# Normalised rows of batches 2 to 7 transposed by DMA instead of by TensorE: attention followed by a normalised MLP, one core of Trainium2

## The chip, the core and the metric

The kernel runs on one core of one Trainium2 chip. A core has TensorE (matmuls and weight loads), DVE (VectorE), ACT (ScalarE), POOL (GpSimd) and SP (SyncE, which issues most of the DMAs). The metric is device time in microseconds of one execution, lower is better. A profiled execution has a span, from its first to its last instruction, and a time of its own that is a little longer.

## The reference, cut to what matters

```
B, H, S, D = 8, 8, 576, 64
scores = q @ k.T / sqrt(D) + min(-(cum_i - cum_j), 0), causal     # cum: running sum of max(s, 0)
attn   = exp(scores - max) / sum
x      = (attn @ v), heads side by side                           # [8, 576, 512]
xn     = (x - mean(x)) / sqrt(var(x) + 1e-6) * g_ln
out    = x + max(xn @ w_ch1, 0) @ w_ch2                           # w_ch1 [512, 2048], w_ch2 [2048, 512]
```

All inputs and the output are float32. The first MLP matmul contracts over the 512 columns of xn, so TensorE needs xn with these columns on the partitions: xn has to be transposed. Attention works in bf16 copies, and so does the MLP.

## The kernel before, in words

**Tiling.** A batch has 576 rows: four tiles of 128 and a rest of 64. The rests of two batches share a tile of 128, so an odd batch has five tiles to normalise and an even batch four; the four shared tiles of all batches make one more chunk of 512 rows at the very end (xTm, "mixed rows"). A tile of xn is [128 rows, 512] in bf16. Its transpose is four blocks of 128 x 128, and for a batch they form xT, [128, 4, 512]: kd counts the blocks of the contraction, the 512 columns are the batch's rows.

**The loop.** One loop runs over n = 8 b + h, batch b and head h (lines 745 to 834). The schedule is written by hand: each engine executes its instructions in the order in which the program lists them. A round n from 16 on does, in order: pre(n), which issues loads, casts and row transposes for later heads; scores(n), matmuls into `sa`, `sb`, `sc` with an exponential on ACT and a causal mask on POOL; one or two units of MLP work with `scores_d` between them; pv(n - 2), attention times v for the head two rounds back; then transposes of xn where the round has them; then further units.

**MLP units.** `queue` holds the MLP of one batch as 32 units: 16 of `mlp1` (line 493: four matmuls `ph` of 128 x 512 that read all 512 columns of xT, followed by a ReLU into hT) and 16 of `mlp2` (four units to a row tile; the fourth ends with `yo` on DVE, line 524, and an output DMA on SP, line 542). The queue is emptied at the end of round 8 b + 3, and the units of batch b - 1 are put in. So the first `ph` of batch b - 1 comes right after the scores of round 8 b + 4, that is of head 4.

**From attention to xT.** Head 7 of batch b - 1 is finished by pv in round 8 b + 1. Then DVE makes the statistics and the tiles xn one after the other (`ln_xn`, line 444; five buffers). In round 8 b + 2 TensorE transposes tiles 0 and 1, in round 8 b + 3 tiles 2 to 4 (`ln_tr`, line 478): four transposes into a PSUM tile `trx` and one copy from there to xT. The copy is on DVE for b = 3 to 7, and on ACT for batch 1 and batch 7. Between the tiles single units run. xT has two buffers, used by turns.

**After the loop.** Batch 7 has its own ending (lines 835 to 842): the last two pv, then for each tile t: xn of tile t + 1, one unit of batch 6, the transposes of tile t. The rest of batch 6's units follow (four), then the MLP of batch 7 and that of the mixed rows, with nothing beside them.

**SP's queue.** SP issues in program order and waits in order. In it stand the loads of v (line 139) and of rows of k and q (line 164), each into one of six staging buffers that a cast on POOL empties; the DMA transposes of these rows into kq (`tr_rows`, line 182), which the scores of batches 3 to 7 read; and the outputs (line 542), each of which waits for its yo. In round 8 b + 2, pre(n) puts one row transpose, four row loads and one v load into it, the units of the round an output; in round 8 b + 3, pre(n) puts four more row loads and a v load.

Of the kernel before, what the change touches and what calls it, by code (L numbers as in the profile page):

```python
# [15 lines left out]
P = 128  # L16
# [3 lines left out]
def kernel(  # L20
# [11 lines left out]
    nc = tc.nc  # L32
    B, H, S, D = q.shape
# [5 lines left out]
    NF = S // P  # L39
# [48 lines left out]
    xTm = const.tile([P, KD, 512], BF16, name="xTm")  # L88
# [7 lines left out]
    def copy_on(eng, out, in_):  # L96
        if eng == "act":
            nc.scalar.copy(out=out, in_=in_)  # L98
        elif eng == "dve":
            nc.vector.tensor_copy(out=out, in_=in_)  # L100
        else:
            nc.gpsimd.tensor_copy(out=out, in_=in_)  # L102
# [27 lines left out]
    def ld_cast_pair(g):  # L130
        ld_cast("k", g)
        ld_cast("q", g)
# [12 lines left out]
    def ld_cast_v(b, t):  # L145
        pn = P if t < NF else TL
        nc.gpsimd.dma_start(
            out=v_bf[b % 2][:pn, t, :, 0:D],
            in_=v[b, :, t * P : t * P + pn, :].rearrange("h s d -> s h d"),
        )  # L150
# [45 lines left out]
    def ld_w1(c):  # L196
        sl = slice(c * 512, (c + 1) * 512)
        nc.gpsimd.dma_start(out=w1_bf[:, :, sl], in_=w1_r[:, :, sl])

    def ld_w2(i):  # L200
        nc.gpsimd.dma_start(
            out=w2_bf[:, 4 * i : 4 * i + 4, :], in_=w2_r[:, 4 * i : 4 * i + 4, :]
        )
# [3 lines left out]
    def aug(gam, eng, h0=0):  # L207
        r = slice(gam * G + h0, gam * G + G)
        i = gam % 2
        eng.dma_start(out=kq[i][D : D + 1, 1, h0:G, 0:S], in_=c_hi[r, :])  # L210
        for j in range(3):
            eng.dma_start(out=kq[i][D + 1 + j : D + 2 + j, 0, h0:G, 0:S], in_=c3[r, j, :])
# [215 lines left out]
    xTs = {}  # L428
    xns = {}
# [48 lines left out]
    def ln_tr(b, t, eng="dve"):  # L478
        if (b, t) not in xns:
            return  # L480
        xn = xns.pop((b, t))
        tr = ps_t.tile([P, KD, P], BF16, name="trx", tag="tr")
        for kd in range(KD):
            nc.tensor.transpose(tr[:, kd, :], xn[:, kd * P : (kd + 1) * P], ident)  # L484
        if t < NF:
            dst = xTs[b][:, :, t * P : (t + 1) * P]
        else:
            dst = xTm[:, :, (b // 2) * P : (b // 2 + 1) * P]
        copy_on(eng, dst, tr)

    first_unit = [False]

    def mlp1(xT, fb):
# [63 lines left out]
    def run_units(n, dve_first=False):  # L557
        for i in range(n):
            if queue:
                first_unit[0] = dve_first and i == 0  # L560
                queue.pop(0)()
# [33 lines left out]
    for i in range(2):  # L595
# [5 lines left out]
        out=maskT,  # L601
        in_=maskT,
# [18 lines left out]
    for t in range(NT):  # L621
# [5 lines left out]
        out=c_in, in0=c_in, scalar1=0.0, scalar2=1.0 / scale, op0=ALU.max, op1=ALU.mult  # L627
    )
    nc.vector.tensor_tensor_scan(
        out=c_sc, data0=c_one, data1=c_in, initial=0.0, op0=ALU.mult, op1=ALU.add  # L630
# [44 lines left out]
    def pre(n):  # L675
        if n == 0:
            nc.vector.memset(mhalf, -0.5)
            ld_cast_pair(4)
        elif n == 1:
            ld_w1(1)  # L680
        elif n == 3:
            ld_cast_pair(5)
            for t in range(NT):
                ld_cast_v(1, t)
        elif n == 4:
            ld_w1(2)
            ld_w1(3)
        elif n == 7:
            ld_cast_pair(6)
            ld_w2(0)  # L690
            ld_cast_pair(7)
            ld_w2(1)
        elif n == 10:
            ld_w2(2)
            ld_w2(3)
        elif n == 12:
            nc.vector.memset(cT[:, :, 0, :, 0], -1.0)
            nc.vector.memset(cT[:, :, 1, :, 1:4], 1.0)
        elif n == 16:
            for r in rows:  # L700
                nc.gpsimd.memset(r[:, :, :, KA:P], 0.0)
        if n in PAIR_LOADS:
            ld_cast_pair(PAIR_LOADS[n])
        if n % 4 == 0 and 2 <= n // 4 + 1 < 2 * NPE:
            aug(n // 4 + 1, nc.sync)
        for gam in range(2 * NPE, NG):
            m = n - 4 * gam
            if m == -6:
                ld_rows(gam, 0), ld_rows(gam, 1)
            elif m == -5:  # L710
                cast_rows(gam, 0), cast_rows(gam, 1)
                ld_rows(gam, 2), ld_rows(gam, 3)
            elif m == -4:
                tr_rows(gam, 0), tr_rows(gam, 1)
                cast_rows(gam, 2), cast_rows(gam, 3)
                ld_rows(gam, 4)
            elif m == -3:
                tr_rows(gam, 2), tr_rows(gam, 3)
                cast_rows(gam, 4)
            elif m == -2:  # L720
                tr_rows(gam, 4)
        for nb in range(2, B):
            m = n - H * nb + (5 if nb == 2 else 7)
            if 0 <= m < NT:
                ld_v(nb, m)
            if 1 <= m <= NT:
                cast_v(nb, m - 1, "pool")
# [16 lines left out]

    for n in range(BH):
        b, h = n // H, n % H
        pre(n)
        if n < 8:
            scores(b, h)
            if h in (1, 3, 5, 6):  # L750
                scores_d(b, h // 2)
            if h in (0, 2, 4):
                qk_pair(h // 2 + 1, ("dve", "dve"), ("act", "dve" if h < 4 else "act"))
            pend.append((b, h))
            if n == 7:
                pv_next()
                tr_pair(4)
                pv_next()
                evac_pair("k", 4, ("act", "act"))
                evac_pair("q", 4, ("act", "act"))  # L760
                trc = bias_tr()
                keep_warm(8)
                continue
            if n % 2 == 1 or n == 0:
                keep_warm(2)
            if n > 1:
                pv_next()
            if n == 6:
                pv_next()
            continue  # L770
        if n == 8:

            phs = [
                pool.tile([P, 512], F32, name="ph", tag=tag)
                for pool, tag in ((ps_m, "m"), (ps_m, "m"), (ps_s, "s"), (ps_s, "s"))
            ]

            def columns(t):
                cols = slice(t * P, (t + 1) * P)
                for fb, ph in enumerate(phs):  # L780
                    for kd in range(KD):
                        nc.tensor.matmul(  # L782
                            ph[:, cols],
                            lhsT=w1_bf[:, kd, fb * P : (fb + 1) * P],
                            rhs=xTs[0][:, kd, cols],
                            start=(kd == 0),
                            stop=(kd == KD - 1),
                        )

            for t in range(NF):  # L790
                ln_tr(0, t, "act" if t < 3 else "dve")
                if t > 0:
                    columns(t - 1)
            columns(NF - 1)
            for fb, ph in enumerate(phs):
                if fb % 2 == 0:
                    nc.scalar.activation(out=hT[:, fb, :], in_=ph, func=ACT.Relu)
                else:
                    nc.vector.tensor_scalar_max(out=hT[:, fb, :], in0=ph, scalar1=0.0)
            ln_first_rstd()  # L800
            queue += batch_units(0)[4:]
            scores(b, h)
            scores_d(b, h // 2)
            pend.append((b, h))
            run_units(1)
            continue

        end = next(m for m in (8 * i + 3 for i in range(2, B + 1)) if m >= n)
        nu = (2 if n < 16 else -(-len(queue) // (end - n + 1))) - 2
        if n in PAIRS:  # L810
            qk_pair(PAIRS[n], ("dve", "dve"), ("act", "act"))
        scores(b, h)
        run_units(1, True)
        if h % 2 == 0:
            scores_d(b, h // 2)
        run_units(1)
        if n > 9:
            pv_next()
        if n == 9:
            bias_rows(trc)  # L820
        pend.append((b, h))
        lt = {2: (0, 1), 3: (2, 3, 4)}.get(h, ()) if b > 1 else ()
        for t in lt:
            ln_tr(b - 1, t, "act" if b == 2 else "dve")
            if t != 1 and t != 4:
                run_units(1)
                nu -= 1
        if n == 2 * H + 2:
            for t in range(3, NT):
                ln_xn(1, t)  # L830
        run_units(nu)
        if b > 1 and h == 3:
            run_units(len(queue))
            queue += batch_units(b - 1)
# [4 lines left out]
    for t in range(NT):  # L839
        ln_xn(B - 1, t + 1)  # L840
        run_units(1)
        ln_tr(B - 1, t, "act")
    run_units(len(queue))
    queue += batch_units(B - 1)
    queue += mixed_units()
# [30 lines left out]
```

## Time and profile before

| what | us |
|---|---|
| median of 3 runs | 368.14 |
| lowest and highest of them | 367.79 and 369.08 |
| the profiled execution's own time | 368.74 |
| its span | 367.0 |
| DMA packets of the span | 147981, 50.42 MB, mean 137 GB/s |

How to read such a profile. The page begins with the busy time of each engine and its share of the span; PEld is TensorE's weight load, which overlaps its matmuls. Then the span is cut into 40 equal slices, with the busy share of each engine in tenths; the row DMA is the mean busy share of the core's 16 DMA engines. "The chain that ended last" follows the end of the program back from instruction to what released it, and gives shares of the span by engine and by line. A group line says: source line, engine, operation, tile written `<-` tile read, count, then durations and where it lies. In a timeline the columns are start, duration (both us), engine, source line, operation; in square brackets stands how long the engine was idle before and what ended that. SPq marks an issue of a DMA on SP: the duration is that of the issue, not of the transfer.

The costliest groups of the page beside those shown further on:

```profile
L515 PE MATMUL py<-w_bf,hT 128*128 128x512 bf16 (+1 forms) x592 | 136.5, 373 | 0.4 <-DVE yo L524 0.4
L497 PE MATMUL ph<-xT,w_bf 128*128 128x512 bf16 x496 | 117.8, 379 | 0.1
```

Both are the MLP. Matmuls are pipelined, so the mean of one (373 and 379 ns) is longer than the distance from one to the next.

### The profile page before, as it was taken

The page shows a single profiled execution, that of the slowest core. Times are in us where ns is not written, and L with a number is a line of the kernel's source. Part 1 is how long each engine was busy: PE and PEld are TensorE (multiplying, and loading weights), DVE is VectorE, ACT ScalarE, POOL GpSimd, SP SyncE. Part 2 cuts the span into 40 slices and gives each one's busy share as a digit, 9 for nine tenths or more (in the row PEclk, how much of TensorE's full clock was granted, in tenths as well). Part 3 has the DMA queues.
Part 4 walks back from the last instruction along what each step waited for, and adds up shares of the span by engine and source line. Part 5 has one row for each costly group of instructions (what it writes and reads, how often), then busy time and mean ns, then how long its engine had stood idle before and what let it go on. Part 6 is the DMA issues. An engine that isn't in the chain of part 4 may idle for free.

```text
span 367.0 us, 8372 instructions
## 1 busy us (share of the span) xinstructions
PE 357.8 (97%) x3079; PEld 198.0 (54%) x3079; DVE 205.8 (56%) x539; ACT 194.2 (53%) x371; POOL 161.3 (44%) x441
## 2 busy tenths in 40 slices
PE   8899999999999999999999999999999999999995
PEld 3577565565555555555555555555555554444444
DVE  7597789796438453944384547743675483112211
ACT  5795988568743674357534753476337522501410
POOL 8864375747553746445754562555652101000000
PEclk9999999999999999999999999999999999999999
DMA  7999995579965989599968996798730011011013
GB/s 138 170 195 175 201 204 88 116 179 173 187 140 129 236 177 189 117 227 184 192 158 203 206 188 133 183 202 183 167 102 2 0 60 57 3 56 58 3 29 86
DMA packets 147981, 50.42 MB, mean 137 GB/s; under 512 B 134185, under 2 KB 143268, under 8 KB 147940
## 3 DMA queue, kind: packets, MB, share of 16 engines
q1 hardware_dynamic: 129364, 40.74, 50.9%
q0 software_dynamic: 18176, 8.62, 20.4%
q10 hardware_dynamic: 400, 0.52, 0.5%
q8 instruction: 24, 0.39, 0.4%
q14 instruction: 17, 0.14, 0.2%
HBM read 37.11 MB, written 9.44 MB: 127 GB/s over the span
## 4 chain that ended last, share of the span: by engine, by line
PE 85%; DVE 7%; ACT 3%; DMA 2%; issue 1%; ACTq 0%
PE ph L497 32%; PE py L515 31%; PE pot L389 7%; PE sc L312 4%; PE sa L312 3%; PE sb L312 3%; DVE xn L451 2%; PE trx L484 2%; ACT er L323 2%; DMA kq<-c 1%; ACT kq L98 1%; PE trqk L255 1%; DVE stats L423 1%; PE ph L782 1%; DMA c_in<-in_s_dram 1%
## 5 line engine op out<-in xcount | busy, mean ns | idle before, releaser
L515 PE MATMUL py<-w_bf,hT 128*128 128x512 bf16 (+1 forms) x592 | 136.5, 373 | 0.4 <-DVE yo L524 0.4
L497 PE MATMUL ph<-xT,w_bf 128*128 128x512 bf16 x496 | 117.8, 379 | 0.1
L507 ACT ACTIVATE hT<-ph 128x512 bf16<-128x512 f32 x102 | 61.0, 598 | 62.8 <-PE ph L497 62.8
L515 PEld LDWEIGHTS <-hT 128*128 128x128 bf16 x592 | 53.5, 98 | 49.1 <-issue 0.9
L497 PEld LDWEIGHTS <-w_bf 128*128 128x128 bf16 x560 | 50.3, 97 | 51.7 <-issue 3.3
L323 ACT ACTIVATE er<-sa 128x512 bf16<-128x512 f32 x64 | 38.2, 597 | 70.3 <-PE sa L312 39.9
L331 POOL TENSOR_SCALAR_AFFINE_SELECT er<-er 128x128 bf16<-128x128 bf16 x216 | 58.2, 294 | 26.4 <-ACT er L323 26.3
L505 DVE TENSOR_SCALAR hT<-ph 128x512 bf16<-128x512 f32 x38 | 26.3, 692 | 54.5 <-PE ph L497 49.1
L176 POOL CAST rows<-rowtmp 128x512 bf16<-128x512 f32 (+1 forms) x50 | 30.5, 609 | 49.1 <-DMA rowtmp<-in_q_dram 48.4
L312 PEld LDWEIGHTS <-kq 68*128 68x128 bf16 x440 | 32.8, 97 | 26.5 <-DMA kq<-c 1.6
L389 PEld LDWEIGHTS <-er 128*128 128x128 bf16 x960 | 37.4, 98 | 14.2 <-issue 0.7
L389 PE MATMUL pot<-v_bf,er 128*128 128x65 bf16 x960 | 39.6, 193 | 0.1
L323 ACT ACTIVATE er<-sc 128x512 bf16<-128x512 f32 x64 | 39.1, 610 | 0.0
L397 DVE RECIPROCAL rinv<-pot 128x5 f32<-128x5 f32 x64 | 12.3, 192 | 47.5 <-PE pot L389 47.2
L323 ACT ACTIVATE er<-sb 128x512 bf16<-128x512 f32 x64 | 38.3, 598 | 0.1
L524 DVE SCALAR_TENSOR_TENSOR yo<-py,rstd,xb 128x512 f32<-128x512 f32 x32 | 23.9, 748 | 25.5 <-PE py L515 20.8
L399 DVE TENSOR_TENSOR xb<-pot,rinv 128x256 f32<-128x256 f32 x64 | 27.2, 425 | 2.2
L439 POOL TENSOR_TENSOR rstd<-rstd,mhalf 128x4 f32<-128x4 f32 (+1 forms) x8 | 8.8, 1097 | 43.8 <-DVE rstd L438 43.8
L312 PE MATMUL sa<-kq 68*128 68x512 bf16 x64 | 24.4, 381 | 1.2 <-DMA kq<-c 1.1
L423 DVE BATCH_NORM_STATS2 stats<-xb 128x6 f32<-128x128 f32 (+2 forms) x100 | 25.3, 312 | 0.4
L312 PE MATMUL sc<-kq 68*128 68x256 bf16 (+1 forms) x208 | 25.2, 232 | 0.3
L102 POOL CAST v_bf<-vtmp 128x512 bf16<-128x512 f32 (+1 forms) x30 | 18.4, 613 | 14.3 <-DMA vtmp<-in_v_dram 14.3
(101 smaller groups left out, 332.8 us busy)
## 6 DMA issues: line engine op xcount, KB each, us to landing
out_dram<-yo SPq DMA_DIRECT2D x32, 256.0 KB
vtmp<-in_v_dram SPq DMA_DIRECT2D x24, 256.0 KB
rowtmp<-in_k_dram SPq DMA_DIRECT2D x40, 128.0 KB
rowtmp<-in_q_dram SPq DMA_DIRECT2D x40, 128.0 KB
w_bf<-in_moe_w_ch_dram POOLq DMA_DIRECT2D x8, 512.0 KB, 11.1
kp<-in_k_dram POOLq DMA_DIRECT2D x11, 144.0 KB, 6.6
qp<-in_q_dram POOLq DMA_DIRECT2D x11, 144.0 KB, 7.3
v_bf<-in_v_dram POOLq DMA_DIRECT2D x8, 128.0 KB, 8.5
```

The source lines that it names most:

```text
L176: nc.gpsimd.tensor_copy(out=r[0:pn, :, :, 0:D], in_=loaded.pop(("rows", gam, t))[0:pn])
L312: nc.tensor.matmul(a[:, c + a0 - q0 : c + a1 - q0], lhsT=k_cols(b, h, kb), rhs=cols, start=True, stop=not (pe_mask and diag),)
L323: nc.scalar.activation(out=e[:, o : o + 512], in_=a, func=ACT.Exp, scale=scale)
L331: nc.gpsimd.affine_select(out=e[:, o : o + P], in_=e[:, o : o + P], compare_op=ALU.is_ge, fill=0.0, base=0, pattern=[[1, P]], channel_mult ...
L389: nc.tensor.matmul(pot[:, t, :], lhsT=e[:, o : o + P], rhs=vv[:, kb, h, :], start=(kb == 0), stop=(kb == last),)
L399: nc.vector.tensor_tensor(out=xb[b][:, :, hs], in0=pot[:, 0:NF, 0:D], in1=rinv[:, 0:NF].unsqueeze(2).to_broadcast([P, NF, D]), op=ALU.mult,)
L423: nc.vector.bn_stats(out=st[b][:, t, part, :], in_=x[:, lo:hi])
L497: nc.tensor.matmul(ph, lhsT=w1_bf[:, kd, fb * P : (fb + 1) * P], rhs=xT[:, kd, :], start=(kd == 0), stop=(kd == KD - 1),)
L505: nc.vector.tensor_scalar_max(out=hT[:, fb, :], in0=ph, scalar1=0.0)
L507: nc.scalar.activation(out=hT[:, fb, :], in_=ph, func=ACT.Relu)
L515: nc.tensor.matmul(py[0], lhsT=hT[:, fb, t * P : (t + 1) * P], rhs=w2_bf[:, fb, c0:c1], start=(fb == 0), stop=(fb == FB - 1),)
L524: nc.vector.scalar_tensor_tensor(out=yo, in0=py[0], scalar=rs, in1=x[:, c0:c1], op0=ALU.mult, op1=ALU.add)
```

## The change

A new helper `ln_dma` does what `ln_tr` does, with one DMA on SP's queue for a tile: it reads xn from SBUF and writes the transpose into xT or xTm, without PSUM and without a copy. The batches 2 to 6 use it in the loop: tiles 0 to 2 at the end of round 8 b + 2, after its units, and tiles 3 and 4 at the start of round 8 b + 3, ahead of pre(n). Batch 7 uses it in the ending, at the place of `ln_tr`. Batches 0 and 1 keep TensorE. The number of units that a round runs is the same; where single units ran between the transposes, they now run in one go.

```diff
+    def ln_dma(b, t):
+        if (b, t) not in xns:
+            return
+        if t < NF:
+            dst = xTs[b][:, :, t * P : (t + 1) * P]
+        else:
+            dst = xTm[:, :, (b // 2) * P : (b // 2 + 1) * P]
+        nc.sync.dma_start_transpose(out=dst, in_=xns.pop((b, t)))
...
     for n in range(BH):
         b, h = n // H, n % H
+        if b > 2 and h == 3:
+            ln_dma(b - 1, 3), ln_dma(b - 1, 4)
         pre(n)
...
-        lt = {2: (0, 1), 3: (2, 3, 4)}.get(h, ()) if b > 1 else ()
+        lt = {2: (0, 1), 3: (2, 3, 4)}.get(h, ()) if b == 2 else ()
         for t in lt:
-            ln_tr(b - 1, t, "act" if b == 2 else "dve")
+            ln_tr(b - 1, t, "act")
...
         run_units(nu)
+        if b > 2 and h == 2:
+            for t in range(3):
+                ln_dma(b - 1, t)
...
     for t in range(NT):
         ln_xn(B - 1, t + 1)
         run_units(1)
-        ln_tr(B - 1, t, "act")
+        ln_dma(B - 1, t)
```

## The prediction, made before the result was known

> **What bounds the kernel now.** I read the page first (busy shares, the slices, the chain that ended last), then the tiles trx and kq, then the timeline around one hand-over from a batch's last output to its next first MLP.
>
> ```profile
> PE 357.8 (97%) x3079; PEld 198.0 (54%) x3079; DVE 205.8 (56%) x539; ACT 194.2 (53%) x371; POOL 161.3 (44%) x441
> ...
> DMA  7999995579965989599968996798730011011013
> ...
> PE 85%; DVE 7%; ACT 3%; DMA 2%; issue 1%; ACTq 0%
> ```
>
> TensorE is busy 97% of the span and holds 85% of the chain: a microsecond taken from its queue is worth about one, and one in which it stands still costs one, since nothing later has slack to give it back. The DMA engines are near 90% in most slices up to three quarters of the span, then nearly idle.
>
> ```profile
> L484 PE MATMUL trx<-ident,xn x144: 217/219/230, 32.1 to 303.1; 128*128 128x128 bf16 x144
> L100 DVE COPY xT<-trx x21: 403/415/425, 35.6 to 271.7; 128x512 bf16<-128x512 bf16 x21
> L98 ACT COPY xT<-trx x11: 586/586/587, 32.6 to 302.3; 128x512 bf16<-128x512 bf16 x11
> ```
> ```profile
> L186 SPq DMA_TRANSPOSE kq<-rows x50: 1222/1274/2432, 83.0 to 267.8; - x50
> ```
>
> The first group is what goes; the second is the nearest thing to what comes: a DMA transpose holds SyncE (SP) about 1.27 us. It is of 1024 columns, and those of 64 rows, half the bytes, take the same (the one at 154.36 below), so the time hangs on the columns or is fixed.
>
> The hand-over of batch 3 (n = 34 to 36), one timeline with all engines:
>
> ```profile
> 150.72 0.39 PE L484 MATMUL trx<-ident,xn 128*128 128x128 bf16 x4
> ...
> 150.95 1.03 PE L515 MATMUL py<-w_bf,hT 128*128 128x512 bf16 x4
> ...
> 153.13 0.75 DVE L524 SCALAR_TENSOR_TENSOR yo<-py,rstd,xb 128x512 f32<-128x512 f32 x1
> ...
> 153.91 0.36 SPq L542 DMA_DIRECT2D out_dram<-yo  x1
> ...
> 154.36 1.23 SPq L186 DMA_TRANSPOSE kq<-rows  x1
> ...
> 156.25 0.50 SPq L164 DMA_DIRECT2D rowtmp<-in_q_dram  x1
> ...
> 157.35 0.51 SPq L164 DMA_DIRECT2D rowtmp<-in_q_dram  x1
> ...
> 157.90 0.51 SPq L139 DMA_DIRECT2D vtmp<-in_v_dram  x1
> ...
> 158.50 0.52 SPq L542 DMA_DIRECT2D out_dram<-yo  x1
> ...
> 159.07 0.43 SPq L164 DMA_DIRECT2D rowtmp<-in_k_dram  x1
> ...
> 159.18 1.03 PE L497 MATMUL ph<-xT,w_bf 128*128 128x512 bf16 x4
> 159.26 0.61 POOL L176 CAST rows<-rowtmp 128x512 bf16<-128x512 f32 x1 [3.10 <-DMA rowtmp<-in_q_dram]
> ...
> 160.54 0.62 POOL L176 CAST rows<-rowtmp 128x512 bf16<-128x512 f32 x1 [0.52 <-DMA rowtmp<-in_q_dram]
> ```
>
> The reader is to see three things. Four transposes of a tile hold TensorE 0.23 us (150.72 to 150.95), well below the 4 x 219 ns of the pipelined records. SP is late: held by the output at 153.91, whose yo DVE makes only after its five xn, it then issues without a pause (transpose, four row loads, one v load, output) until 159.02. And the first ph, which reads all 512 columns of xT, stands at 159.18. A load issued by 156.75 is there at 159.26 and one issued by 157.86 at 160.54: 2.5 to 2.7 us after the end of its issue, with the queue full.
>
> ```profile
> 157.90:162.50 4.60, 4.60 (x46) 2.62 (x45) 2.73 (x7) 2.33 (x6) 1.96 (x5) 1.00 1.00 248
> ...
> 269.70:275.00 5.30, 5.30 (x59) 3.20 (x58) 3.11 (x7) 1.77 (x5) 1.43 (x7) 1.00 0.28 102
> ```
>
> By stretches (the last two columns are the DMA share and GB/s): at this hand-over the DMA engines are full at 248 GB/s; at that of batch 6 they are not.
>
> [...] The trace shows the cold rate at its start, 12 matmuls in 5.13 us, 0.43 us each against 0.22 later (4 in 0.86 in the chain):
>
> ```profile
> 1.27 5.13 PE L568 MATMUL idle<-zeros 128*128 128x512 bf16 x12 [1.27 <-DVE warm L584]
> ```
>
> **The change part by part.** Tiles moved: batches 2, 4, 6 have four, 3, 5, 7 have five: 27.
>
> 1. Removed from TensorE: 27 x 4 transposes, 27 x 0.22 = 5.9 us, all on the path. Removed elsewhere: 22 copies of 0.415 us on DVE and 5 of 0.59 on ACT, beside TensorE and worth nothing by themselves (DVE is busy 56%, ACT 53%).
>
> 2. Added to SP: 27 transposes of 512 columns. Unknown duration d: 0.61 us if it goes by columns (half of 1.22), 1.27 if fixed. I take the middle, 0.95; nothing argues for an end. Bytes: 131 KB each, at 248 GB/s 0.53 us of all DMA engines, rounded up to 0.57.
>
> 3. Moved: in the loop, all five come after the output of head 2 in program order, so at 159.07 in this hand-over (call it S), in front of the row and v loads of head 3. With a full queue the work ahead is worth 2.6 us; it shrinks while SP issues more slowly than the engines drain. The fourth transpose lands at S + 4d + max(0.85, 2.6 - 4(d - 0.57)). The 0.85 is my floor: the output issued at 153.91 shows its first bytes at about 154.75 in the DMA slices. With d = 0.95: S + 4.88. With 0.61 also S + 4.88, as the engines then set the pace; with 1.27, S + 5.93.
>
> 4. The new wait: the first ph of the batch. Behind it on TensorE stands everything, in order, and the engine has nothing else to run. What this costs is landing less ph of before, and the removed transposes no longer count, for TensorE would only come to the wait earlier:
>
> | batch | S | first ph before | landing | cost |
> |---|---|---|---|---|
> | 2 | 119.83 | 120.86 | 124.71 | 3.85 |
> | 3 | 159.07 | 159.18 | 163.95 | 4.77 |
> | 4 | 197.30 | 196.90 | 202.18 | 5.28 |
> | 5 | 235.14 | 235.23 | 240.02 | 4.79 |
> | 6 | 270.25 | 272.95 | 274.90 | 1.95 |
>
> S and ph are read as above from the same view of each hand-over; batch 6 has no load left, so its landing is S + 3.8 + 0.85. Sum: +20.6 us.
>
> 5. Batch 7: SP comes to its transposes after the output of the yo at 299.03, about 300.2. Four issues end at 304.0, landing 304.85. TensorE, 5 x 0.22 = 1.1 us ahead of the 306.63 of before, wants it at 305.5. No wait: -1.1 us. The fifth goes to the mixed rows, needed much later. With d = 1.27 the landing is 306.1, and the gain 0.5.
>
> 6. The clock. The stalls are the costs above plus the 0.9 to 1.1 us that TensorE arrives early: 4.7, 5.9, 6.2, 5.9, 2.8. [...] some 2.7 drops. Each costs half of some 4.8 us in which the start of this trace ran cold (eleven of the twelve at 0.43): 2.4 us, as an estimate. +6.4, between 0 and 12.
>
> 7. SP's later loads and rows come 5d = 4.75 us later. TensorE is then as late as that, so this cover holds; if the stall vanished, the casts on POOL, with the masks of head 4 behind them, would be late instead.
>
> Sum on the profiled execution: 368.74 + 20.6 - 1.1 + 6.4 = 394.6. That execution is 0.6 above the median of 368.14, so **394 us**.
>
> **The rivals.**
> - Hidden transposes, faster: if they land before TensorE comes, only part 1 is left: 368.1 - 5.9 = 362. For it: TensorE is the bound, DVE gets 9 us back. Against it: with arrival 1 us earlier, four issues and a landing would have to fit within 0 us (batches 2 to 5) or 1.8 (batch 6). It decides when SP comes to its transposes some 5 us sooner than the outputs let it.
> - Half hidden: S + 2 to 3 us instead of 4.88, no cold clock, so 2 to 3 us less on each of four, and batch 6 without a stall: 374 to 378. For it: the transposes might be issued faster than any of the 50 seen.
> - The full DMA queue becomes the bound: 22 x 0.57 = 12.5 us more of it, pushing rows, casts and masks behind TensorE's stalls: 394 + 12 = 406. For it: share 1.00 in these stretches. Against it: gaps, and the stalls give the queue that time back.
>
> **How the numbers follow.** Stalls as worked out 0.73; hidden 0.07; half hidden 0.08; DMA-bound 0.12. Range from the first case: low end d = 0.61 and the 0.85 floor without backlog, 12.9 - 1.1, 380; high end d = 1.27, 26.1 - 0.5, and all five clock drops, 12: 406. This leaves out the hidden cases and a little of the others. About 0.3% is what a measurement tells from no change here. Faster 0.07, within it 0.02, slower 0.91.
>
> **What would show it.** Right: the waits list TensorE (or its weight load, L507) behind a DMA of xT, five times 3 to 6 us, and none for batch 7; the transposes of xT on SP last 0.6 to 1.3 us and start just after head 2's output; granted clock below 1.00 in some slices after 120 us. Wrong: ph directly after the scores at each hand-over; or TensorE's new idle time before pot with masks late on POOL, which is the third rival.

## The result, and the profile after

The changed kernel takes 406.23 us (median of 4 runs, 405.35 to 408.09) against 368.0 us before (4 runs): a ratio of 1.104, 95% interval 1.099 to 1.108. The prediction had the direction and the wait that causes most of the loss, but said 394 with 406 as its upper end. The profiled execution takes 405.35 us, its span is 403.6.

The page of the changed kernel, the lines that answer to those of before:

```profile
PE 358.2 (89%) x2924; PEld 194.4 (48%) x2971; DVE 197.2 (49%) x517; ACT 192.4 (48%) x366; POOL 161.7 (40%) x441
...
PEclk9999999999996999879996999979996999999999
DMA  8999993799668895789968994888942003201002
...
PE 53%; SPq 11%; DMA 10%; POOL 8%; issue 8%; DVE 5%; ACT 4%; POOLq 0%; ACTq 0%; DVEq 0%
```

TensorE is busy 89% of the span instead of 97%, and holds 53% of the chain instead of 85%. SyncE's issues (SPq), which the page of before does not list, hold 11%, DMAs 10% instead of 2%. The row PEclk has five dips, where that of before has none: the clock is halved five times, for 6.83 us each. The transposes add 3.5 MB of DMA traffic (53.95 MB against 50.42), but over the longer span the mean is no higher, 134 GB/s against 137.

The waits of TensorE in the changed kernel (total us, times, longest), and the DMA transposes on SyncE as the tile xT lists them (ns, shortest, median, longest):

```profile
PE ph L507 <- DMA xT<-xn: 31.7, 6, 7.6
PE py L525 <- DVE yo L534: 1.3, 2, 0.7
```
```profile
L499 SPq DMA_TRANSPOSE xT<-xn x24: 1216/1264/1287, 119.3 to 340.9; - x24
```

The wait that the prediction named is there for each of the batches 2 to 6, two of them, of 7.6 us, well above the 3 to 6 us that it gave, and a sixth of 1.0 us stands before batch 7, where it had said none. And a transpose of 512 columns holds SyncE 1.264 us, as long as one of 1024 (1.274 us in the kernel before).

The first hand-over (batch 2) in the chain of waits, start and duration in us:

```profile
118.72 0.52 SPq L552
...
119.29 1.25 SPq L499
...
120.59 1.26 SPq L499
...
121.89 1.26 SPq L499
...
123.20 2.37 DMA xT<-xn
...
125.61 1.89 PE ph L507 x4
```

The output of head 2 is issued, the four transposes follow one by one, the fourth lands 2.37 us after the start of its issue, and ph starts, 6.3 us after the start of the first issue. The "x4" with 1.89 us is the other thing to see: four matmuls of 512 columns take 0.86 us at full clock, in the chain of before. The stretches around this hand-over (columns: stretch, length, then busy time of PE, PEld, DVE, ACT and POOL, PEclk, DMA share, GB/s):

```profile
119.58:121.51 1.93, 0.01 (x1) 0.00 (x0) 0.14 (x1) 1.24 (x3) 1.08 (x4) 1.00 1.06 295
121.51:125.61 4.10, 0.00 (x0) 0.00 (x0) 0.00 (x0) 0.00 (x0) 1.61 (x5) 0.50 0.60 119
125.61:128.34 2.73, 2.73 (x9) 1.07 (x10) 0.69 (x1) 0.27 (x1) 0.34 (x1) 0.50 0.84 191
128.34:131.00 2.66, 2.61 (x26) 1.48 (x26) 0.91 (x3) 1.20 (x2) 1.89 (x6) 1.00 1.02 245
```

The clock drops 1.9 us into the wait and stays at half for 6.8 us, 2.7 of them with work. The same stretches of the other hand-overs give 3.1, 2.7, 3.3 and 5.9 us of work at half clock.

So the span's 36.6 us add up: five waits of 6.0, 7.6, 6.2, 7.6 and 3.2 us (30.7), one of 1.0 before batch 7's ph, half of 17.7 us of slow work (8.8), less the 5.9 of removed transposes: 34.6. Some 2.0 us remain in small waits, 0.8 of them of scores on the last row transpose of kq and 0.9 of py on yo (1.3 against 0.4 before).

### The profile page after: what moved, and what is told of

Same layout as the page of the kernel before. It is cut to its first block, busy times and chain, and to the rows that moved or that the text cites. A ratio compares the mean times of both kernels' runs of the same rounds, so it can differ in the third digit from the quotient of the medians.

```text
span 403.6 us, 8147 instructions
## 1 busy us (share of the span) xinstructions
PE 358.2 (89%) x2924; PEld 194.4 (48%) x2971; DVE 197.2 (49%) x517; ACT 192.4 (48%) x366; POOL 161.7 (40%) x441
## 2 busy tenths in 40 slices
DMA packets 162668, 53.95 MB, mean 134 GB/s; under 512 B 148873, under 2 KB 157956, under 8 KB 162628
## 4 chain that ended last, share of the span: by engine, by line
PE 53%; SPq 11%; DMA 10%; POOL 8%; issue 8%; DVE 5%; ACT 4%; POOLq 0%; ACTq 0%; DVEq 0%
PE ph L507 27%; PE py L525 13%; SPq L499 5%; SPq L164 5%; PE pot L389 4%; DMA rowtmp<-in_q_dram 3%; DMA xT<-xn 3%; POOL er L331 2%; PE sc L312 2%; DMA vtmp<-in_v_dram 2%; PE sb L312 2%; PE sa L312 2%; ACT er L323 2%; DMA v_bf<-in_v_dram 2%; POOL rstd L439 1%
## 5 line engine op out<-in xcount | busy, mean ns | idle before, releaser
L507 PE MATMUL ph<-xT,w_bf 128*128 128x512 bf16 x476 | 124.4, 397 | 33.2 <-DMA xT<-xn 31.7
L525 PE MATMUL py<-w_bf,hT 128*128 128x512 bf16 (+1 forms) x570 | 131.2, 373 | 2.5 <-DVE yo L534 1.3
L507 PEld LDWEIGHTS <-w_bf 128*128 128x128 bf16 x560 | 51.8, 100 | 88.0 <-issue 33.0
L358 ACT ACTIVATE er<-sd 64x128 bf16<-64x128 f32 x32 | 8.9, 278 | 35.5 <-PE sd L347 35.5
```

Source lines behind the costliest of these rows:

```text
L507: nc.tensor.matmul(ph, lhsT=w1_bf[:, kd, fb * P : (fb + 1) * P], rhs=xT[:, kd, :], start=(kd == 0), stop=(kd == KD - 1),)
L525: nc.tensor.matmul(py[0], lhsT=hT[:, fb, t * P : (t + 1) * P], rhs=w2_bf[:, fb, c0:c1], start=(fb == 0), stop=(fb == FB - 1),)
```

## The experiments

Theory A: the loss comes from SyncE's queue, where the transposes stand late and take long to issue. Theory B: the bound is the DMA engines' load. The times of before, measured with them, were 368.1 to 368.4 us. Behind each time stands its ratio to before, with the 95% interval. The expectation of the added transposes uses the letters otherwise: its A is the wait of ph alone, its B is SyncE's time and the DMA traffic together.

### Idle work in place of the wait

```diff
         scores(b, h)
+        if b > 2 and h == 4:
+            keep_warm(14 if b == 7 else 28)
         run_units(1, True)
```

> The changed kernel with 28 matmuls of zeros (14 for batch 6) between the scores of head 4 and the first ph: TensorE does idle work where it stood waiting, about 6.0 us (3.0) of the 6.0 to 7.6 (3.2), so the landing of xT is not put off. If the clock drops cost what their busy part says (half of 2.7, 3.1, 2.7, 3.3 and 5.9 us, together 8.8 us), the granted clock stays at 1.00 and the time falls to 396 to 399 us. If the drops cost nothing, because something else sets the pace after the stall, it stays at 405 to 407 us.

Measured: 396.54 us, 1.077 (1.075 to 1.079), granted clock 1.000 over the whole span. In its timeline the idle work fills what was the wait, and the four matmuls after it are fast again:

```profile
120.11 6.21 PE L578 MATMUL idle<-zeros 128*128 128x512 bf16 x27
126.32 1.04 PE L507 MATMUL ph<-xT,w_bf 128*128 128x512 bf16 x4
```

The halved clock was worth 9.7 us of the 38, about what its busy part says (8.8). The waits themselves remain, filled with idle work but for 4.9 us in which ph still waits for xT.

### The transposes added to the kernel before, read by nobody

```diff
+    ghost = const.tile([P, NT, KD, P], BF16, name="ghost")
+    ghosts = {}
...
+    def ln_ghost(b, t):
+        if (b, t) in ghosts:
+            nc.sync.dma_start_transpose(out=ghost[:, t, :, :], in_=ghosts.pop((b, t)))
...
         xns[b, t] = xn
+        if b > 1:
+            ghosts[b, t] = xn
...
         b, h = n // H, n % H
+        if b > 2 and h == 3:
+            ln_ghost(b - 1, 3), ln_ghost(b - 1, 4)
         pre(n)
```

The other calls stand where the change has `ln_dma`; TensorE's transposes stay.

> The kernel before, with TensorE's transposes kept, and the same 27 DMA transposes added at the places where the change has them, written to a tile that nobody reads. SyncE and the DMA engines carry all that the change gives them, but no ph waits for it. Theory A (the loss is the wait of ph): 368 to 371 us, at most some delay of casts and masks on POOL. Theory B (DMA traffic and SyncE's time are the loss): 380 us or more.

Measured: 385.64 us, 1.048 (1.045 to 1.051). I had expected A's number, and it is not near. No ph waits for xT here, so the 17.5 us come from what the transposes do to SyncE's queue and to the DMA engines. TensorE's longest sum of waits, POOL's timeline at the hand-over of batch 3, and below it TensorE's:

```profile
PE pot L389 <- POOL er L331: 9.5, 6, 3.1
```
```profile
172.34 0.61 POOL L176 CAST rows<-rowtmp 128x512 bf16<-128x512 f32 x1 [7.00 <-DMA rowtmp<-in_q_dram]
...
175.24 1.03 POOL L331 TENSOR_SCALAR_AFFINE_SELECT er<-er 128x128 bf16<-128x128 bf16 x4
```
```profile
175.58 1.29 PE L389 MATMUL pot<-v_bf,er 128*128 128x65 bf16 x15 [3.09 <-POOL er L331]
```

The row loads behind the five issues come late, POOL stands 7.0 us before a cast, the causal masks queue behind the cast, and attention times v waits for a mask. Each of the two waits of 3 us comes with a drop of the clock (granted clock 0.984 over the span), which is part of the 17.5 us. That is the cover which part 7 of the prediction named for SyncE's later loads: in the changed kernel POOL stands 6.1 us before the same cast (at 176.46), but TensorE is late by as much and no pot waits for a mask; here it isn't late. Whether SyncE's time or the bytes cause it, this run doesn't tell.

### Two tiles to a transpose, at the same place

```diff
+        src = xns.pop((b, t))
+        if t < NF and t % 2 == 0:
+            return
         if t < NF:
-            dst = xTs[b][:, :, t * P : (t + 1) * P]
+            dst = xTs[b][:, t - 1 : t + 1, :, :].rearrange("p t k s -> p (t k) s")
+            src = xnw[b, t // 2].rearrange("p t c -> p (t c)")
         else:
-            dst = xTm[:, :, (b // 2) * P : (b // 2 + 1) * P]
-        nc.sync.dma_start_transpose(out=dst, in_=xns.pop((b, t)))
+            dst = xTm[:, b // 2, :, :]
+        nc.sync.dma_start_transpose(out=dst, in_=src)
```

xT becomes [128, 4 tiles, 4 blocks, 128] for this, and a buffer of xn holds two tiles (three such buffers, and one for the mixed rows, instead of five of one tile); those lines are left out here.

> The changed kernel with two tiles to a DMA transpose (1024 columns instead of 512; xT laid out tile by tile), so two issues instead of four in front of ph, at the same place in SyncE's queue and with the same bytes. Theory A with a cost that is fixed per issue (1.26 us for 512 columns as for 1024): landing 2.5 us earlier at each hand-over, waits of 3.5 to 5 us in batches 2 to 5 and below 1 us in batch 6, fewer or equal clock drops: 386 to 393 us. If the issue goes by columns, or the engines' drain sets the pace: an issue of 2.5 us, waits as before, 403 us or more.

Measured: 397.68 us, 1.081 (1.077 to 1.084), between the two answers. The issue is nearly fixed, the tile view says:

```profile
L512 SPq DMA_TRANSPOSE xT<-xn x12: 1231/1359/1747, 119.2 to 330.6; - x12
```

Twice the columns take 1.36 us instead of 1.26. But in batches 2 to 5 ph came only 1.0 to 1.6 us earlier, 4.75 us after the start of the first issue in batch 2 (119.19 to 123.94) and 5.16 to 5.42 in the others. The prediction's formula gives S + 4.88 for this case, with the loads ahead of the transposes setting the pace (S is the moment at which SyncE reaches the first transpose). That fits, but isn't shown by itself: in batch 6, with no load ahead, ph still came 1.7 us after the end of the second issue, against 1.1 to 1.4 us with single tiles, so a part belongs to the larger transpose. The clock still dropped four times.

### The transposes right behind xn

```diff
             for t in range({1: 3, B - 1: 1}.get(pb, NT)):
                 ln_xn(pb, t)
+                if 1 < pb < B - 1:
+                    ln_dma(pb, t)
```

The calls of rounds 8 b + 2 and 8 b + 3 go away; in the ending, `ln_dma(B - 1, t)` stands before `ln_xn(B - 1, t + 1)`.

> The same 27 DMA transposes, but each put on SyncE's queue right after its xn is made (round 8b+1 for batches 2 to 6, ahead of the unit in batch 7's ending), so ahead of the output, the row transpose and the five loads. In the trace of before SyncE stands idle here (148.6 to 153.9 us) and DVE ends the fifth xn at 153.0. Theory A (place in SyncE's queue: the transposes were late because of what stood in front of them): they land near 155.6 against a first ph at 158 to 159, no wait of ph longer than 0.5 us, clock 1.00 after the start, and the 5.9 us of removed TensorE work become visible: 362 to 364 us. Theory B (the full DMA queue is the bound, wherever the transposes stand): 375 us or more, with casts and masks late on POOL. Theory C (a DMA transpose lands too slowly to be used at all here): the five waits stay above 3 us, 390 us or more.

Measured: 377.72 us, 1.026 (1.024 to 1.028). The five waits of ph are gone, and the time is outside A's range all the same. It lies in B's, but the late masks that B named are not among TensorE's waits. SyncE's timeline shows why, and TensorE's what it costs (batch 3):

```profile
150.89 5.21 SPq L499 DMA_TRANSPOSE xT<-xn  x4
156.19 1.79 SPq L499 DMA_TRANSPOSE xTm<-xn  x1
158.08 0.53 SPq L552 DMA_DIRECT2D out_dram<-yo  x1
158.70 1.25 SPq L186 DMA_TRANSPOSE kq<-rows  x1
```
```profile
161.41 0.40 PE L312 MATMUL sb<-kq 68*128 68x64 bf16 x3 [2.66 <-DMA kq<-rows]
```

Five issues take from 150.89 to 157.98, where before SyncE was idle until 153.91. The last row transpose for head 4, at 154.36 before, starts at 158.70, and now the scores of head 4 wait for it: five waits on TensorE, 8.3 us together, and three drops of the clock. The wait has moved to the next thing in SyncE's queue.

### Early, and then fewer issues, or another order

The first version moves that row transpose in front of the early ones and keeps single tiles; the second takes two tiles to a transpose; the third does both.

```diff
             elif m == -3:
                 tr_rows(gam, 2), tr_rows(gam, 3)
                 cast_rows(gam, 4)
-            elif m == -2:
+                if gam % 2 == 1:
+                    tr_rows(gam, 4)
+            elif m == -2 and gam % 2 == 0:
                 tr_rows(gam, 4)
```

> The early place with single tiles, and the last row transpose for head 4 moved in front of them (one round earlier, its rows are cast by then). Theory A: the waits of the scores for kq are gone, no clock drop; output and loads stand behind four or five issues and come some 1 to 3 us late, which casts on POOL partly absorb: 363 to 368 us. Theory B: 374 us or more, with the wait turning up elsewhere.

> The early place with two tiles to a transpose: two issues of about 1.3 us (three in odd batches) stand in front of the output and the last row transpose of head 4's k and q, instead of four (five). In the run with the early place this row transpose came 3 to 4 us late and the scores of head 4 waited for it (8.3 us in five waits on TensorE, three clock drops). Theory A (SyncE's issue time in a chain, moved from one consumer to the next): SyncE is back at the row transpose 2.5 us sooner, the waits of the scores shrink below 1 us each, no clock drop, 362 to 366 us. Theory B (the DMA engines' load is the bound): 374 us or more as with the early place, since the bytes are the same.

> Both of these: two tiles to a transpose, early, and the row transpose in front. Theory A: all that SyncE holds up is gone, and what is left is the 5.9 us of removed TensorE work less what DVE's yo holds: 362 to 364 us. Theory B: 374 us or more.

Measured: 374.06 us, 1.015 (1.012 to 1.018), for the first; 367.88 us, 0.999 (0.997 to 1.001), for the second; 365.58 us, 0.993 (0.991 to 0.995), for the third. All three miss theory A's ranges, the second and third by less than 2 us; the first just reaches the 374 us that theory B had said. In it, waits of ph (2.2 us), of py on yo (2.0) and of pot on masks (2.0) are left; in the second, two waits of the scores, one of them of 1.5 us where at most 1 had been expected. The second moves the same bytes as the early place in three issues instead of five (two instead of four in even batches), and is 9.8 us faster. The DMA traffic of the early place and then that of pairs there:

```profile
DMA packets 162668, 53.95 MB, mean 143 GB/s; under 512 B 148873, under 2 KB 157956, under 8 KB 162628
```
```profile
DMA packets 162283, 53.94 MB, mean 147 GB/s; under 512 B 148489, under 2 KB 157572, under 8 KB 162244
```

The waits of the scores, in the same order (total us, times, longest):

```profile
PE sb L312 <- DMA kq<-rows: 8.3, 5, 2.7
```
```profile
PE sb L312 <- DMA kq<-rows: 2.8, 2, 1.5
```

Bytes and packets are the same within 0.3%. The first and the third version differ by pairs in the same way, and by 8.5 us. So the number of issues on SyncE decides and not the load of the DMA engines; theory B falls. The third version even keeps the DMA engines busier than the kernel before (a share of 0.93 to 1.00 in the five stretches of the loop from 82.5 to 272 us, against 0.78 to 0.91), and is faster than it by 0.7%; of TensorE's waits in it only three exceed 1 us in total, the last of them at the very start:

```profile
PE sa L312 <- DMA kq<-c: 1.5, 1, 1.5
PE py L538 <- DVE yo L547: 1.3, 2, 0.7
PE idle L591 <- DVE warm L607: 1.3, 1, 1.3
```

### The ending alone, and two controls of the fastest version

The first of these keeps TensorE in the loop and has only batch 7's `ln_dma`, as in the change.

> Only batch 7's five tiles by DMA, as in the change; the loop keeps TensorE. Theory A: in the changed kernel the wait of 1.0 us there ate the 1.1 us saved, so 367.7 to 368.7 us, no change that can be told. If the ending had its part in the loss (the transposes behind the outputs), 370 us or more.

Measured: 368.69 us, 1.001 (1.000 to 1.002), no difference that can be told. The second takes the fastest version's moved row transpose and its layout of xT, and leaves all transposes of xn on TensorE; the third is the fastest version with batch 7's on TensorE.

> A control without any DMA transpose of xn: the kernel before with the row transpose of head 4 one round earlier and xT laid out tile by tile, as in the fastest version so far. If that version's 0.7% come from the DMA transposes, this is 367.5 to 369 us; if they come from the moved row transpose or the layout, 365 to 366 us.

> Two tiles to a transpose, early, row transpose in front, but batch 7 by TensorE as before. The ending alone by DMA moved nothing that can be told, so both theories that leave it out of the account say 365 to 366.5 us; if the ending gains 1.1 us by DMA here, 366.5 us or more; if the chain over SyncE's outputs costs there, below 365 us.

Measured: 368.15 us, 0.9995 (0.998 to 1.001), and 367.14 us, 0.996 (0.994 to 0.998). So the gain of the fastest version comes from its DMA transposes and not from the moved row transpose or the layout; its larger buffers of xn were in no control. Some 1.4 us of the gain seem to come from the ending (0.993 against 0.996 of before), where pairs issued early would pay and the transposes of the change did not; but the two intervals overlap, so this part is weakly shown.

## Why the prediction was wrong in size

By its own steps, on the profiled execution (394.6 predicted, 405.35 measured):

- **Part 1**, what goes: right in sign, and the sum above closes with it. Alone it was never measured: in the fastest version less than half of the 5.9 us is left by the medians (368.2 to 365.6), and 3.3 us by the profiled spans (367.0 to 363.7). There some 1.7 us went to longer waits of TensorE (py on yo 1.3 against 0.4, sa on kq 1.5 against 1.1, pot on a mask 0.4 against none); the rest is open.
- **Part 2**, the issue, is the step that failed. It took d = 0.95 us, the middle between "by columns" and "fixed"; the 24 issues measured 1.264 (median), and the pairs 1.36 for twice the columns. It is nearly fixed, the upper end. So four issues held SyncE 5.14 to 5.21 us, short gaps included, and not 3.8, at all five hand-overs together 6.9 us more. The profile of before held a hint, no proof: transposes of 64 rows took 1.22 to 1.27 us, and the median of all 50, most of them of 128 rows, was 1.27, which speaks for a fixed time but leaves the columns open. Nor is an issue a finished transpose: the fourth tile of batch 2 landed 2.37 us after the start of its issue. That the bytes of a transpose cost what 248 GB/s makes of them was the author's estimate, and no run showed it by itself.
- **Part 3**, landing: the floor of 0.85 us after the last issue was 1.1 to 1.4 us. Together with part 2, ph started 6.3 to 6.6 us after S and not 4.9 (4.65 in batch 6). The other arm of the formula, the loads ahead draining in S + 4.88, agrees with the pairs of batches 2 to 5 (4.75 to 5.42), though not all of that time need be the loads.
- **Part 4**, the wait and its place: right, batch by batch. The waits sum to 30.7 us against the 25.5 of the prediction's gaps. The later landings make 7.9 of difference (1.4 to 1.7 in each; 6.9 of it is part 2), and 2.7 came back because SyncE reached the transposes of batches 4 and 6 some 1.3 to 1.5 us sooner, against TensorE, than read from before; the output issue of 1.87 us that had held it in batch 4 took 0.63. That was luck for the prediction: without it the miss would be some 13 us.
- **Part 5**, batch 7: the wait of 1.0 us ate the gain, -0.1 instead of -1.1. It is the same step: ph came 6.4 us after the start of the first issue, where 4.65 had been counted. The 0.5 that it named for d = 1.27 was too much as well.
- **Part 6**, the clock: five drops instead of 2.7, each costing some 1.8 us instead of 2.4; 8.8 us by the trace and 9.7 by the experiment, against 6.4. The number of 2.7 was the author's estimate and rested on nothing that the profile of before shows. In the changed kernel each of the five waits had its drop: that at batch 6 came 2.25 us into a wait of 3.2 us, and that at batch 2 only 1.9 us into its wait of 6.0.
- **Part 7**, the cover of the later loads: right, and borne out by the added transposes, which cost 17.5 us where nothing covers them. In the changed kernel it held but for some of the 2.0 us that remain.

The sum of the misses is 5.2 (waits), 1.0 (ending), 2.4 (clock) and 2.0 (the rest), 10.6 of 10.75. The rival of a full DMA queue would have met 406, but not by its reason: at the early place, fewer issues with the same bytes took the loss away. The hidden case can be had, but only with the transposes at another place and joined in pairs.

Open: how the 17.5 us of the added transposes divide between issue time and the bytes ahead of the loads. A run with pairs in that place wasn't tried.

## What to carry to other kernels

Here a DMA that replaced work of the bound engine was priced by the queue that issued it (four issues held SyncE for 5.14 to 5.21 us): count the issues, what stands in front of them, and what stands behind them and who waits for that. Moving it earlier handed the wait to the next in the queue, and then fewer and larger issues helped more (9.8 us) than another order (3.7 us). And with the early place waits of 2.06 and 2.66 us on TensorE cost more than themselves, because the clock went with them: 3.41 us of work at half clock behind the second, some 1.7 us more.

## What the runs showed of the hardware

- The issue of a DMA transpose on SyncE hardly depends on its size: 1.22 to 1.27 us for 64 rows of 1024 columns in the kernel before; by the medians of the runs, 1.22 to 1.26 for 128 rows of 512 and 1.25 to 1.36 for 128 of 1024.
- TensorE's clock was halved also where TensorE had stood still for only 2.06 us: with the early place, behind such a wait that ended at 202.20, four matmuls of 512 columns that started at 203.74 took 1.89 us, against 1.03 at full clock in the same kind of view. In the changed kernel it fell 1.9, 3.9, 2.1, 4.1 and 2.25 us into a wait and stayed at half for 6.83 us each time. The starts of these drops lie 47.79, 44.37, 47.79 and 44.37 us apart, which is 14, 13, 14 and 13 times 3.413 us, half the length of a drop: in this trace every drop began on one grid of that step. In the last 3.41 us ahead of the drop at batch 2, TensorE still worked for 1.49 us. With the early place, a wait of 2.66 us ending at 161.41 was followed by a drop from 162.45 to 165.86, a microsecond after the work had resumed:

```profile
162.45:165.86 3.41, 3.41 (x24) 1.81 (x23) 0.69 (x1) 1.40 (x4) 1.53 (x4) 0.50 0.98 251
166.00:168.00 2.00, 2.00 (x13) 0.99 (x12) 0.67 (x3) 0.92 (x2) 1.53 (x5) 1.00 1.11 244
```

  In the changed kernel each of the five waits of TensorE of 3.2 to 7.6 us came with a drop. With pairs at the same place there were four drops for five waits of ph (23.1 us together, the longest 6.1; granted clock 0.965), with the added transposes one for each of the two waits of 3 us (0.984), with the early place three for five waits of the scores (8.3 us together, the longest 2.7; 0.986). Waits of 1.0 us before batch 7's ph, of 1.5 us with pairs early, and one of 1.9 us behind the idle work came with none. Where a limit lies, and whether a wait's place in the grid matters, these runs don't show.
